# Weighing 64 of 128 value rows on ScalarE and GpSimd in a decode-attention kernel

## The chip, the core and the metric

The kernel runs on one core of a Trainium2 chip. The metric is the device time of one execution, in microseconds, as the median of three runs. The profiler recorded one execution, and every time quoted here comes from its page, its trace or from the times of the runs. Engines go by the profile's names: PE is TensorE, DVE is VectorE, ACT is ScalarE, POOL is GpSimd, SP is SyncE, which issues the loads.

## What is computed

One decoding step of an attention block with adaptive layer norms, followed by a small feed-forward block. Batch 4, one query per sequence, 32 heads of 128, 4096 cached positions, model width 512, feed-forward width 1792, all float32. The caches of keys and values are by far the largest inputs.

```
mod = (silu(c) @ w_mod).reshape(B, 6, 1, -1)          # sa, ca, ga, sb, cb, gb
h = layernorm(x) * (1 + ca) + sa
q = (h @ wq), split into 32 heads
scores = einsum("bhqd,bhkd->bhqk", q, k_cache) * Dh ** -0.5
p = softmax(scores)
o = einsum("bhqk,bhkd->bhqd", p, v_cache)
x = x + ga * (o @ wo)
h = layernorm(x) * (1 + cb) + sb
x = x + gb * (silu(h @ w1) @ w2)
```

## The kernel before

**Tiles.** A step `n` (0 to 31) handles one batch entry `b = n % 4` and a group `t = n // 4` of four heads. Its key tile and its value tile are 128 partitions by 128 rows by 128 columns (`NJ = 128`, `Dh = 128`): a partition holds 128 positions of one head, so each tile is 64 KiB per partition, 8.39 MB in all.

**Slots and loads.** All big tiles go through one pool, `kv`, with three slots taken in turn (class `Slot`). SP issues every load (`fetch`, L85), in the order of the program: key 0, key 1, value 0, key 2, value 1, key 3 and so on. So the load of key `n+2` takes the slot of value `n-1` and waits until that tile has been used up, and the load of value `n+1` takes the slot of key `n+1` and waits until DVE has reduced it.

**One step.** There is no scheduler: each engine's order is the order in which the loop (L434 to L475) is written, and semaphores do the rest.

- `mult`: the key tile is multiplied by the query, 40 rows on POOL and 88 on DVE (L280). DVE reads the query from PSUM, POOL a copy in SBUF that ACT makes (`make_qb`, L275).
- `vmult(n-1)`: of the value tile of the step before, POOL weighs the first 32 rows (`NV = 32`, L323) with the softmax weights in `sc` and adds them to four rows by halving (L327).
- `pv(n-1)`: PE handles the other 24 groups of four rows with weights that were placed in `pz` (L348), accumulating in `po`.
- `red`: DVE sums the products of the key tile along the columns (L285), 88 rows and then the 40 of POOL. This ends the use of the key tile.
- `rowmax`, `bmax`, `negmax`: the maximum per partition, then per head through a transpose on PE into a PSUM tile `mx`; DVE reduces it into a small SBUF tile `hx` (L298), masks it (L299) and sums it (L301).
- `vsum(n-1)`: PE adds POOL's four rows to `po` (L333). This ends the use of the value tile.
- `softexp(n)`: ACT takes the exponentials (L307) with their sums in `rs`, and POOL spreads the weights over `pz[0]` and `pz[1]` (L311).
- On the fourth step of a group (`b == 3`), `gather` (L359, L365) and `norm` follow: PE sums the denominators (L383 or L392) behind `vsum`, and DVE inverts them (L386, L387 in groups 0 to 3, L394 to L397 in groups 4 to 7). `gather(t-1, 1)` and `spread(t-1)` come on the second and third steps of the next group; `spread` ends with a copy into `oz` (L415) in groups 4 to 7.

The last two value tiles (`first(n) == 0`) go to PE whole. After the last step come the output projection (L423, L428), the second layer norm and the feed-forward block (L506, L516).

Of the kernel before, what the change touches and what calls it, by code (L numbers as in the profile page):

```python
# [9 lines left out]
F32 = mybir.dt.float32  # L10
AF = mybir.ActivationFunctionType
ALU = mybir.AluOpType
AX = mybir.AxisListType
# [4 lines left out]
def kernel(  # L18
# [10 lines left out]
    nc = tc.nc  # L29
    P = 128  # L30
    B, H, S, Dh = kc.shape
# [3 lines left out]
    W = P // G  # L35
    HP = 4
# [3 lines left out]
    TA = NT // 2  # L40
    QA = P // (HP * TA)
    RA = Dh // QA
    NJ = HP * S // P
    JJ = 4
    NG = NJ // JJ
    HG = NG // 2
# [4 lines left out]
    FG = F // G  # L51
    NA = 40
    NL = 56
    NV = 32
    SCALE = 1.0 / math.sqrt(Dh)
    EPS = 1e-5
    N = B * NT
# [4 lines left out]
    work = ctx.enter_context(tc.tile_pool(name="work", bufs=2))  # L62
# [3 lines left out]
    def psum(shape, tag, bufs):  # L66
        return ps.tile(shape, F32, tag=tag, name=tag, bufs=bufs)
# [19 lines left out]
    kt, vt = {}, {}  # L87
# [34 lines left out]
    ident = const.tile([P, P], F32, name="ident")  # L122
# [54 lines left out]
    oz = const.tile([P, NT - TA, R, B], F32, name="oz")  # L177
# [65 lines left out]
    for k in range(NK):  # L243
        for ch in range(H * Dh // CW):
            i, g = divmod(ch, G)
# [31 lines left out]
    sc, nm, po, rs = {}, {}, {}, {}  # L277
# [11 lines left out]
        nc.vector.tensor_reduce(nm[n], sc[n], axis=AX.X, op=ALU.max)  # L289

    def bmax(n):
        p = psum([P, P], "mx", 2)
        nc.tensor.transpose(p, nm[n].to_broadcast([P, P]), ident)  # L293
        nm[n] = p

    def negmax(n):
        m = work.tile([P, HP], F32, tag="hx", name=f"hx{n}")
        nc.vector.tensor_reduce(m, nm[n].rearrange("p (i x) -> p i x", i=HP), axis=AX.X, op=ALU.max)  # L298
        nc.vector.tensor_mul(m, m, hn)  # L299
        nm[n] = work.tile([P, 1], F32, tag="nm", name=f"nm{n}")  # L300
        nc.vector.tensor_reduce(nm[n], m, axis=AX.X, op=ALU.add)  # L301

    def softexp(n):
        t, b = divmod(n, B)
        if b == 0:
            rs[t] = work.tile([P, B], F32, tag="rs", name=f"rs{t}")
        nc.scalar.activation(sc[n], sc[n], AF.Exp, bias=nm[n], accum_out=rs[t][:, b : b + 1])  # L307
        for h in range(2):
            f = first(n) if h == 0 else 0
            m = HG - f  # L310
            nc.gpsimd.tensor_mul(  # L311
                pz[h][:, f * W : HG * W].rearrange("p (g x) -> p g x", g=m)[:, :, E:].rearrange("p g (i j) -> p g i j", i=HP),
                sc[n][:, JJ * (HG * h + f) : HG * JJ * (h + 1)].rearrange("p (g j) -> p g j", j=JJ)
                .unsqueeze(2).to_broadcast([P, m, HP, JJ]),
                hm.unsqueeze(1).unsqueeze(3).to_broadcast([P, m, HP, JJ]),
            )

    def first(n):
        return NV // JJ if n < N - 2 else 0

    def vmult(n):
        if first(n):
            nc.gpsimd.tensor_mul(  # L323
                vt[n][:, :NV, :], vt[n][:, :NV, :], sc[n][:, :NV].unsqueeze(2).to_broadcast([P, NV, Dh])
            )
            for m in (NV // 2, NV // 4, JJ):
                nc.gpsimd.tensor_add(vt[n][:, :m, :], vt[n][:, :m, :], vt[n][:, m : 2 * m, :])  # L327

    def vsum(n):
        t, b = divmod(n, B)  # L330
# [46 lines left out]
    rd = {}  # L377

    def norm(t):
        p = psum([P, B], "mx", 2)  # L380
        if t < TA:
            g = slice(W * t, W * (t + 1))
            nc.tensor.matmul(p[g], b8.rearrange("p i x -> p (i x)"), rs[t], start=True, stop=True)  # L383
            rd[t] = work.tile([P, B, QA], F32, tag="ra", name="ra", bufs=1)
            m = work.tile([P, B], F32, tag="dx", name="dx")
            nc.vector.reciprocal(m[g], p[g])  # L386
            nc.vector.tensor_mul(  # L387
                rd[t][g], m[g].unsqueeze(2).to_broadcast([W, B, QA]),
                dqm[g].unsqueeze(1).to_broadcast([W, B, QA]),
            )  # L390
            return
        nc.tensor.matmul(p, blk.rearrange("p i x -> p (i x)"), rs[t], start=True, stop=True)  # L392
        m = work.tile([P, B], F32, tag="dx", name="dx")
        nc.vector.tensor_mul(m, p, xm)  # L394
        rd[t] = work.tile([P, 2], F32, tag="rd", name="rd")
        nc.vector.tensor_reduce(rd[t][:, 0:1], m, axis=AX.X, op=ALU.add)
        nc.vector.reciprocal(rd[t][:, 1:2], rd[t][:, 0:1])  # L397

    def spread(t):
        if t < TA:  # L400
            g = slice(W * t, W * (t + 1))
            v = work.tile([P, B, QA, RA], F32, tag="o", name="v", bufs=1)
            nc.vector.tensor_mul(
                v[g], od[t][g].rearrange("p b (q r) -> p b q r", q=QA),
                rd[t][g].unsqueeze(3).to_broadcast([W, B, QA, RA]),
            )
            nc.vector.tensor_reduce(oa[g], v[g].rearrange("p b q r -> p r b q"), axis=AX.X, op=ALU.add)
            return
        on = work.tile([P, R, QW], F32, tag="lnu", name="on", bufs=1)
        nc.vector.tensor_scalar(  # L410
            on, od[t].rearrange("p (x r) -> p r x", r=R), rd[t][:, 1:2], None, op0=ALU.mult
        )
        ot = work.tile([P, R, W], F32, tag="o", name="ot", bufs=1)
        nc.vector.transpose(ot, on)
        nc.vector.tensor_copy(oz[:, t - TA], ot[:, :, :B])  # L415

    accp = psum([P, D], "acc", 1)
    nc.vector.memset(accp, 0.0)
# [15 lines left out]
    for n in range(N):  # L434
        t, b = divmod(n, B)
# [5 lines left out]
        w, m = (NJ // 2, NL // 2) if n == 0 else (NJ, NL) if n == 1 else (NJ, NA)  # L441
        for lo in range(0, NJ, w):
            mult(nc.gpsimd, qw, n, lo, lo + m)
            mult(nc.vector, qb, n, lo + m, lo + w)
            if n + 1 < N and not lo:
                make_qb(n + 1)
            if n:
                vmult(n - 1)
                pv(n - 1)
            red(n, lo + m, lo + w)  # L450
# [4 lines left out]
        else:  # L455
# [6 lines left out]
            fetch(s2.t, w12, 0, 3 * F, *(NK * F + i * D for i in (0, 5, 8, 10, 11, 12, 13, 14)))  # L462
        rowmax(n)
        bmax(n)
        if n and first(n - 1):
            vsum(n - 1)
        negmax(n)
        softexp(n)
        if b == 3:
            gather(t, 0)  # L470
            norm(t)
        if t and b == 1:
            gather(t - 1, 1)
        if t and b == 2:
            spread(t - 1)  # L475
    pv(N - 1)
    gather(NT - 1, 1)
    spread(NT - 1)
    project_a()
    project(TA, NT)  # L480
# [84 lines left out]
```

## Time and profile before

| What | Value |
|---|---|
| Median of three runs | 1319.33 us (1319.29 to 1319.63) |
| Profiled execution | 1319.24 us |
| Its span | 1317.5 us |
| Busy: DVE, POOL, PE, ACT | 1029.0, 848.6, 381.3, 51.4 us |
| Moved | 567.65 MB, 431 GB/s over the span |
| Granted PE clock, mean | 0.611 |

The profile's timelines give for each instruction its start and its length in microseconds, the engine, the line of the kernel, what it writes and reads, and in brackets how long the engine stood idle before it and what released it. The groups by shape give the count after an `x`, then the busy time, the mean length in ns, and the idle time ahead with its releasers. The rows of the windows give, for a stretch of time, the busy time of PE, its weight loads, DVE, ACT and POOL with the number of instructions, then the granted PE clock, the busy share of the DMA engines and the rate in GB/s.

### The profile page before, as it was taken

The page shows a single profiled execution, that of the slowest core. Times are in us where ns is not written, and L with a number is a line of the kernel's source. Part 1 is how long each engine was busy: PE and PEld are TensorE (multiplying, and loading weights), DVE is VectorE, ACT ScalarE, POOL GpSimd, SP SyncE. Part 2 cuts the span into 40 slices and gives each one's busy share as a digit, 9 for nine tenths or more (in the row PEclk, how much of TensorE's full clock was granted, in tenths as well). Part 3 has the DMA queues.
Part 4 walks back from the last instruction along what each step waited for, and adds up shares of the span by engine and source line. Part 5 has one row for each costly group of instructions (what it writes and reads, how often), then busy time and mean ns, then how long its engine had stood idle before and what let it go on. Part 6 is the DMA issues. An engine that isn't in the chain of part 4 may idle for free.

```text
span 1317.5 us, 5429 instructions
## 1 busy us (share of the span) xinstructions
PE 381.3 (29%) x2114; PEld 104.2 (8%) x2114; DVE 1029.0 (78%) x361; ACT 51.4 (4%) x164; POOL 848.6 (64%) x227
## 2 busy tenths in 40 slices
PE   3402333221222232133222123232312332221357
PEld 0100000000000000000000001000000000000013
DVE  2597788987877888788888887789887888977852
ACT  1100000000000000000000000000000000000001
POOL 0457767666876766687676677667667767666800
PEclk9756666655666665566665566666556666555668
DMA  9999999999999999999999999999999999999998
GB/s 414 436 422 446 434 424 442 422 440 442 420 442 432 432 438 434 434 436 428 436 438 430 430 440 434 430 436 438 426 438 438 428 432 438 434 432 438 428 428 344
DMA packets 11433, 567.65 MB, mean 431 GB/s; under 512 B 1280, under 2 KB 1296, under 8 KB 2192
## 3 DMA queue, kind: packets, MB, share of 16 engines
q1 hardware_dynamic: 11408, 567.31, 99.5%
q8 instruction: 17, 0.28, 0.1%
q14 instruction: 8, 0.07, 0.0%
HBM read 567.30 MB, written 0.01 MB: 431 GB/s over the span
## 4 chain that ended last, share of the span: by engine, by line
DMA 58%; DVE 25%; POOL 12%; PE 4%; issue 1%; ACT 0%; DVEq 0%; SPq 0%; POOLq 0%; ACTq 0%
DMA k<-in_A_k_cache_dram 31%; DMA v<-in_A_v_cache_dram 25%; DVE sc L285 14%; DVE k L280 10%; POOL v L327 6%; POOL v L323 5%; DMA wq<-in_A_wq_dram 3%; PE po L333 1%; PE po L348 1%; PE q L246 1%; PE acc L423 0%; PE q L506 0%; PE acc L428 0%; PE po L516 0%; PE mx L256 0%
## 5 line engine op out<-in xcount | busy, mean ns | idle before, releaser
L285 DVE TENSOR_REDUCE sc<-k 128x88 f32<-128x11264 f32 (+3 forms) x66 | 553.1, 8422 | 3.2
L280 DVE TENSOR_TENSOR k<-k,q 128x11264 f32<-128x11264 f32 (+2 forms) x33 | 376.3, 11402 | 169.8 <-DMA k<-in_A_k_cache_dram 155.5
L280 POOL TENSOR_TENSOR k<-k,qw 128x5120 f32<-128x5120 f32 (+2 forms) x33 | 361.8, 10964 | 123.5 <-DMA k<-in_A_k_cache_dram 92.1
L348 PE MATMUL po<-v,pz 128*32 128x512 f32 x1568 | 243.6, 786 | 645.4 <-DMA v<-in_A_v_cache_dram 645.4
L323 POOL TENSOR_TENSOR v<-v,sc 128x4096 f32<-128x4096 f32 x30 | 211.1, 7036 | 241.5 <-DMA v<-in_A_v_cache_dram 241.5
L327 POOL TENSOR_TENSOR v<-v 128x2048 f32<-128x2048 f32 (+2 forms) x90 | 243.5, 2705 | 7.1
L348 PEld LDWEIGHTS po<-v,pz 128*32 128x32 f32 x1568 | 64.7, 140 | 831.7 <-issue 831.7
L333 PE MATMUL po<-v,hs 128*32 128x512 f32 x60 | 57.4, 1060 | 140.6 <-POOL v L327 140.6
L311 POOL TENSOR_TENSOR pz<-sc,hm 128x128 f32<-128x128 f32 (+1 forms) x64 | 31.5, 514 | 33.7 <-ACT sc L307 33.7
L293 PE MATMUL mx<-ident,rm 128*128 128x128 f32 x32 | 11.3, 352 | 115.0 <-DVE rm L289 115.0
L307 ACT ACTIVATE sc<-sc,nm 128x128 f32<-128x128 f32 x32 | 12.8, 402 | 712.9 <-DVE nm L301 712.9
L275 ACT ACTIVATE qw<-q 128x128 f32<-128x128 f32 x32 | 8.9, 278 | 450.5 <-DVE k L280 417.4
L359 DVE TENSOR_TENSOR o<-po,jm 128x512 f32<-128x512 f32 x16 | 10.9, 682 | 14.6 <-PE po L348 14.6
L298 DVE TENSOR_REDUCE hx<-mx 128x4 f32<-128x128 f32 x32 | 9.3, 292 | 16.4 <-PE mx L293 16.4
L333 PEld LDWEIGHTS po<-v,hs 128*32 128x32 f32 x60 | 5.5, 141 | 147.3 <-POOL v L327 147.3
L365 DVE TENSOR_REDUCE s<-o 128x128 f32<-128x512 f32 x16 | 16.5, 1033 | 0.6
L299 DVE TENSOR_TENSOR hx<-hx,hn 128x4 f32<-128x4 f32 x32 | 16.0, 501 | 1.1
L293 PEld LDWEIGHTS mx<-ident,rm 128*128 128x128 f32 x32 | 4.7, 148 | 143.3 <-issue 112.3
L271 PE MATMUL q<-qm,blk 128*128 128x512 f32 x16 | 15.5, 1068 | 1.7 <-ACT qm L269 1.7
L199 PE MATMUL q<-wm 128*32 128x512 f32 x48 | 9.5, 698 | 18.9 <-DVE wm L183 18.9
L386 DVE RECIPROCAL dx<-mx 32x4 f32<-32x4 f32 x4 | 0.7, 179 | 16.7 <-PE po L333 11.9
L394 DVE TENSOR_TENSOR dx<-mx,xm 128x4 f32<-128x4 f32 x4 | 0.6, 162 | 15.7 <-PE mx L392 15.7
(113 smaller groups left out, 168.8 us busy)
## 6 DMA issues: line engine op xcount, KB each, us to landing
k<-in_A_k_cache_dram SPq DMA_DIRECT2D x2, 4096.0 KB, 51.9
wm<-in_head_dram SPq DMA_DIRECT2D x1, 6160.0 KB, 17.7
wo<-in_A_wo_dram SPq DMA_DIRECT2D x1, 4096.0 KB, 19.0
wo<-in_A_wo_dram SPq DMA_DIRECT2D x1, 3072.0 KB, 25.8
w<-in_B_w_dram SPq DMA_DIRECT2D x1, 2688.0 KB, 33.7
w<-in_B_w_dram SPq DMA_DIRECT2D x1, 1280.0 KB, 38.0
wo<-in_A_wo_dram SPq DMA_DIRECT2D x1, 1024.0 KB, 27.9
w<-in_B_w_dram SPq DMA_DIRECT2D x4, 256.0 KB, 17.5
```

The lines of the kernel that those rows point to most:

```text
L246: nc.tensor.matmul(pq[i][W * g : W * (g + 1), :], hT[:, k, :], wqt[:, k, ch * CW : (ch + 1) * CW], start=k == 0, stop=k == NK - 1,)
L271: nc.tensor.matmul(p, blk.rearrange("p i x -> p (i x)"), m, start=True, stop=True)
L280: eng.tensor_mul(kt[n][:, lo:hi, :], kt[n][:, lo:hi, :], src[n].unsqueeze(1).to_broadcast([P, hi - lo, Dh]))
L285: nc.vector.tensor_reduce(sc[n][:, lo:hi], kt[n][:, lo:hi, :], axis=AX.X, op=ALU.add)
L293: nc.tensor.transpose(p, nm[n].to_broadcast([P, P]), ident)
L299: nc.vector.tensor_mul(m, m, hn)
L311: nc.gpsimd.tensor_mul(pz[h][:, f * W : HG * W].rearrange("p (g x) -> p g x", g=m)[:, :, E:].rearrange("p g (i j) -> p g i j", i=HP), sc[n ...
L323: nc.gpsimd.tensor_mul(vt[n][:, :NV, :], vt[n][:, :NV, :], sc[n][:, :NV].unsqueeze(2).to_broadcast([P, NV, Dh]))
L327: nc.gpsimd.tensor_add(vt[n][:, :m, :], vt[n][:, :m, :], vt[n][:, m : 2 * m, :])
L333: nc.tensor.matmul(po[t, q][0:W, :], hs[:, o : o + W], vt[n][:, :JJ, :].rearrange("p j d -> p (j d)"), start=False, stop=a == 1,)
L348: nc.tensor.matmul(po[t, q][W * g : W * (g + 1), :], pz[h][:, o : o + W], vt[n][:, JJ * j : JJ * (j + 1), :].rearrange("p j d -> p (j d)") ...
L365: nc.vector.tensor_reduce(s, o.rearrange("p j d -> p d j"), axis=AX.X, op=ALU.add)
```

## The change

`NV` goes from 32 to 64. For thirty value tiles ACT now weighs rows 16 to 63, one row per instruction and in place (48 of 128x128), POOL rows 0 to 15 in one instruction. POOL then adds the seven further blocks of eight rows to the first, each in turn, and last the two halves of that block. PE keeps rows 64 to 127, 16 groups instead of 24. With 64 rows gone, `pz[0]` is not filled for these tiles. The small tile of the maximum becomes four more columns of the PSUM tile `mx`, the inverse of the denominators is written over the denominators in PSUM, and the copy into `oz` goes from DVE to ACT.

```diff
-    NV = 32
+    NV = 64
+    NC = 8
+    NP = 16
...
     def bmax(n):
-        p = psum([P, P], "mx", 2)
-        nc.tensor.transpose(p, nm[n].to_broadcast([P, P]), ident)
+        p = psum([P, P + HP], "mx", 2)
+        nc.tensor.transpose(p[:, :P], nm[n].to_broadcast([P, P]), ident)
         nm[n] = p
 
     def negmax(n):
-        m = work.tile([P, HP], F32, tag="hx", name=f"hx{n}")
-        nc.vector.tensor_reduce(m, nm[n].rearrange("p (i x) -> p i x", i=HP), axis=AX.X, op=ALU.max)
+        m = nm[n][:, P:]
+        nc.vector.tensor_reduce(m, nm[n][:, :P].rearrange("p (i x) -> p i x", i=HP), axis=AX.X, op=ALU.max)
...
         for h in range(2):
-            f = first(n) if h == 0 else 0
+            f = min(max(first(n) - HG * h, 0), HG)
             m = HG - f
+            if not m:
+                continue
...
     def vmult(n):
         if first(n):
+            v = vt[n]
+            for j in range(NP, NV):
+                nc.scalar.activation(v[:, j, :], v[:, j, :], AF.Copy, scale=sc[n][:, j : j + 1])
             nc.gpsimd.tensor_mul(
-                vt[n][:, :NV, :], vt[n][:, :NV, :], sc[n][:, :NV].unsqueeze(2).to_broadcast([P, NV, Dh])
-            )
-            for m in (NV // 2, NV // 4, JJ):
-                nc.gpsimd.tensor_add(vt[n][:, :m, :], vt[n][:, :m, :], vt[n][:, m : 2 * m, :])
+                v[:, :NP, :], v[:, :NP, :], sc[n][:, :NP].unsqueeze(2).to_broadcast([P, NP, Dh])
+            )
+            for lo in range(NC, NV, NC):
+                nc.gpsimd.tensor_add(v[:, :NC, :], v[:, :NC, :], v[:, lo : lo + NC, :])
+            nc.gpsimd.tensor_add(v[:, :JJ, :], v[:, :JJ, :], v[:, JJ:NC, :])
...
-            m = work.tile([P, B], F32, tag="dx", name="dx")
-            nc.vector.reciprocal(m[g], p[g])
+            nc.vector.reciprocal(p[g], p[g])
             nc.vector.tensor_mul(
-                rd[t][g], m[g].unsqueeze(2).to_broadcast([W, B, QA]),
+                rd[t][g], p[g].unsqueeze(2).to_broadcast([W, B, QA]),
...
-        nc.vector.tensor_copy(oz[:, t - TA], ot[:, :, :B])
+        nc.scalar.activation(oz[:, t - TA], ot[:, :, :B], AF.Copy)
```

The changed kernel's lines stand two further down from `NP` on, and seven further from `norm` on. POOL's order in the fourth step of a group, before: one key tile's part, the value tile, the placement of the weights, the next key tile's part.

```order
L280 TENSOR_TENSOR k_643<-k_643,qw_655 128x5120 [waits DMAHW2_49]
L323 TENSOR_TENSOR v_688<-v_688,sc_645 128x4096 [waits DMAHW3_49]
L327 TENSOR_TENSOR v_688<-v_688 128x2048 [waits Pool_49]
L327 TENSOR_TENSOR v_688<-v_688 128x1024 [waits Pool_49]
L327 TENSOR_TENSOR v_688<-v_688 128x512 [waits Pool_49]
L311 TENSOR_TENSOR pz_113<-sc_720,hm 128x8x16 [waits PE_49,Activation_49]
L311 TENSOR_TENSOR pz_114<-sc_720,hm 128x16x16 [waits PE_49]
L280 TENSOR_TENSOR k_718<-k_718,qw_723 128x5120 [waits DMAHW4_49]
```

The same place after the change:

```order
L282 TENSOR_TENSOR k_898<-k_898,qw_910 128x5120 [waits DMAHW2_49]
L330 TENSOR_TENSOR v_988<-v_988,sc_900 128x2048 [waits DMAHW3_49,DVE_49]
L334 TENSOR_TENSOR v_988<-v_988 128x1024 [waits Pool_49]
L334 TENSOR_TENSOR v_988<-v_988 128x1024 [waits Activation_49,Pool_49] x6
L335 TENSOR_TENSOR v_988<-v_988 128x512 [waits Pool_49]
L315 TENSOR_TENSOR pz_114<-sc_1017,hm 128x16x16 [waits PE_49,Activation_49]
L282 TENSOR_TENSOR k_1015<-k_1015,qw_1020 128x5120 [waits DMAHW4_49]
```

Six of the eight additions now wait for ACT as well as for the addition before, and one placement of weights is left. ACT's order at the same place before, where the exponential follows the copy of the query:

```order
L275 ACTIVATE qw_655<-q 128x128 [waits PE_49,Pool_49]
L307 ACTIVATE sc_645,rs_523<-sc_645,nm_698 128x128 [waits DVE_49,Pool_49]
L369 ACTIVATE mz<-s,am 128x128 [waits DVE_49,Activation_49]
L369 ACTIVATE mz<-s,am 128x128
L275 ACTIVATE qw_723<-q 128x128 [waits DVE_49,Pool_49]
L307 ACTIVATE sc_720,rs_767<-sc_720,nm_765 128x128 [waits DVE_49,Pool_49]
```

And after, with the value tile's 48 scalings ahead of each exponential:

```order
L277 ACTIVATE qw_910<-q 128x128 [waits PE_49,Pool_49]
L329 ACTIVATE v_882<-v_882,sc_802 128x128 [waits DMAHW6_49,DMAHW1_49,Activation_49]
L329 ACTIVATE v_882<-v_882,sc_802 128x128 x47
L309 ACTIVATE sc_900,rs_693<-sc_900,nm_997 128x128 [waits DVE_49,Pool_49]
L377 ACTIVATE mz<-s,am 128x128 [waits DVE_49,Activation_49]
L377 ACTIVATE mz<-s,am 128x128
L277 ACTIVATE qw_1020<-q 128x128 [waits DVE_49,Pool_49]
```

The exponential and the two scalings for `gather` stand behind a wait for the value tile. PE at the end of the fourth step before:

```order
L293 MATMUL mx<-ident,rm_690 128x128 [waits DVE_49,PE_49]
L333 MATMUL po<-v_625,hs 32x512 [waits Pool_49]
L370 MATMUL od<-mz,s_124 32x256 [waits PE_49,Activation_49]
L383 MATMUL mx<-rs_523,b_120 32x4 [waits PE_49]
L348 MATMUL po<-v_688,pz_113 32x512 [waits DMAHW3_49,Pool_49]
```

It is the same after, but for the names and that the value groups begin with `pz_114`: the denominators (L383, now L391) stand behind L333, now L341, which waits for POOL. On SP the order of the loads is the same; a key load now waits for ACT besides PE.

## The prediction

> **What bounds the kernel now.** I read the page first: the span, the busy shares and the DMA queues.
>
> ```profile
> span 1317.5 us, 5429 instructions
> PE 381.3 (29%) x2114; PEld 104.2 (8%) x2114; DVE 1029.0 (78%) x361; ACT 51.4 (4%) x164; POOL 848.6 (64%) x227
> q1 hardware_dynamic: 11408, 567.31, 99.5%
> 60.00:1240.00 1180.00, 313.32 (x1587) 79.70 (x1587) 969.46 (x281) 38.06 (x136) 826.88 (x214) 0.59 1.00 434
> ```
>
> No engine is full, but the loading queue is busy 99.5% of the span; the last row, from the table of windows, shows DMA share 1.00 and 434 GB/s from 60 to 1240 us. So compute costs time only where it makes a load start so late that the queue runs dry. The kernel streams 32 key and 32 value tiles through three slots, so the question is how early each load is issued. SP's timeline around the fourth tile of a head group, then GpSimd's, ScalarE's and DVE's rows from theirs:
>
> ```profile
> 493.57 0.33 SPq L85 DMA_DIRECT2D v<-in_A_v_cache_dram  x1
> 500.95 0.33 SPq L85 DMA_DIRECT2D k<-in_A_k_cache_dram  x1
> 532.25 0.33 SPq L85 DMA_DIRECT2D v<-in_A_v_cache_dram  x1
> ...
> 483.57 7.04 POOL L323 TENSOR_TENSOR v<-v,sc 128x4096 f32<-128x4096 f32 x1 [8.27 <-DMA v<-in_A_v_cache_dram]
> 490.68 8.27 POOL L327 TENSOR_TENSOR v<-v 128x2048 f32<-128x2048 f32 x3
> 502.94 11.03 POOL L280 TENSOR_TENSOR k<-k,qw 128x5120 f32<-128x5120 f32 x1 [3.06 <-DMA k<-in_A_k_cache_dram]
> 522.24 7.04 POOL L323 TENSOR_TENSOR v<-v,sc 128x4096 f32<-128x4096 f32 x1 [8.28 <-DMA v<-in_A_v_cache_dram]
> ...
> 495.49 0.40 ACT L307 ACTIVATE sc<-sc,nm 128x128 f32<-128x128 f32 x1 [30.96 <-DVE nm L301]
> ...
> 493.57 0.29 DVE L289 TENSOR_REDUCE rm<-sc 128x1 f32<-128x128 f32 x1
> ...
> 501.04 0.18 DVE L386 RECIPROCAL dx<-mx 32x4 f32<-32x4 f32 x1 [3.98 <-PE po L333]
> 501.26 0.18 DVE L387 TENSOR_TENSOR ra<-dx,dqm 32x32 f32<-32x32 f32 x1
> 502.95 11.89 DVE L280 TENSOR_TENSOR k<-k,q 128x11264 f32<-128x11264 f32 x1 [1.51 <-DMA k<-in_A_k_cache_dram]
> 514.94 17.28 DVE L285 TENSOR_REDUCE sc<-k 128x88 f32<-128x11264 f32 x2
> ...
> 541.59 11.89 DVE L280 TENSOR_TENSOR k<-k,q 128x11264 f32<-128x11264 f32 x1 [7.51 <-DMA k<-in_A_k_cache_dram]
> ```
>
> Call the landing of a value tile T: GpSimd starts it at 483.57. A key tile lands at T+19.4 (502.95), the next value tile at T+38.7 (522.24). Two loads wait on compute:
>
> - The key load at 500.95 needs the slot of the value tile of T, so it waits for GpSimd's sums and PE's last matmul (L333). It stands behind the value load issued at 493.57, whose bytes land at 522.24. So it is issued 21.3 us before the queue could run dry.
> - The value load at 532.25 needs DVE's last reduction of a key tile. The transfer ahead of it lands at 541.59, so its lead is 9.3 us. This is the tight one, and DVE sets it.
>
> How much lead does a transfer need? An upper and a lower bound come from the first and the last DMA of the kernel:
>
> ```profile
> wm<-in_head_dram SPq DMA_DIRECT2D x1, 6160.0 KB, 17.7
> out_dram<-w SPq DMA_DIRECT2D x1, 8.0 KB, 1.8
> ```
>
> The 8 KB one takes 1.8 us from issue to landing. The head's 6.31 MB at 434 GB/s would take 14.5 us and takes 17.7, so 3.2 us lie around it. A lead of over 3.2 us costs nothing; between 1.8 and 3.2 it is open. I take 1.8: nothing else is on the queue for that DMA, while the head's 3.2 holds the kernel's own start.
>
> **The change, part by part.** Durations come from the groups kept apart by shape:
>
> ```profile
> L323 POOL TENSOR_TENSOR v<-v,sc 128x4096 f32<-128x4096 f32 x30 | 211.1, 7036 | 241.5 <-DMA v<-in_A_v_cache_dram 241.5
> L327 POOL TENSOR_TENSOR v<-v 128x1024 f32<-128x1024 f32 x30 | 70.3, 2344 | 2.4
> L327 POOL TENSOR_TENSOR v<-v 128x512 f32<-128x512 f32 x30 | 37.9, 1263 | 2.4
> L269 ACT ACTIVATE qm<-qn,sel 128x128 f32<-128x128 f32 x32 | 10.2, 389 | 8.2 <-DVE oa L407 4.8 <-DVE oz L415 3.3
> L299 DVE TENSOR_TENSOR hx<-hx,hn 128x4 f32<-128x4 f32 x32 | 16.0, 501 | 1.1
> L394 DVE TENSOR_TENSOR dx<-mx,xm 128x4 f32<-128x4 f32 x4 | 0.6, 162 | 15.7 <-PE mx L392 15.7
> ```
>
> GpSimd, per value tile. Before: 7.04 + 0.07 + 8.27 = 15.4 us. After: 16 rows weighed, half of 7.04, 3.5; seven additions of 128x1024 at 2.344, 16.4; one of 128x512, 1.3; eight gaps of 0.07, 0.6. Together 21.8 us, 6.4 more. The smaller placement of the weights (one multiplication, not two) stands behind it.
>
> ScalarE, per value tile: 48 scalings of 128x128. L269 is the same operation with a column as its scale: 10.2 us busy for 32, so 0.319 each back to back, 15.3 us; alone 0.389, 18.7 us. GpSimd takes eight rows every 2.4 us and first works 5.9 us on its own 16, so its last addition of eight could begin at T+18.1; the last rows are ready at T+15.3, or T+18.7 at the slow end. The sums then end at T+21.8, or 18.7+2.34+0.07+1.26 = T+22.4. I take 21.8, since the scalings stand together as in L269's busy time. A lower end: none of GpSimd's rows can go faster than the same shapes went, so 21.8 it is.
>
> What waits for that? The exponential (L307) stands behind the 48 on ScalarE: T+11.9 (495.49) becomes T+15.3 to 18.7, still ahead of GpSimd's end, and only the placement of weights and the denominators need it. GpSimd's part of the next key tile starts at about T+22.6, not T+19.4, and ends at T+33.7; DVE needs it after 11.9 + 11.9 us of its own work, at T+43. GpSimd is free five us before the next value tile (T+38.7). The key load moves from T+17.4 to T+23.8, and its lead from 21.3 to 14.9 us: far above 3.2. SP's queue is otherwise in the same order, and the loads behind it were issued later in any case.
>
> PE: 16 groups for 24, off the path. The scratch tiles in PSUM: L299 takes 0.50 us on two SBUF operands, L394 0.16 with one in PSUM, so some 0.34 x 32 = 11 us of DVE go, all after the reduction that releases the load: zero on the path (between 0 and the same 0.34 late, if PSUM gave nothing). The copy of `oz` moves to ScalarE. The one near the end of the kernel, from its timeline:
>
> ```profile
> 1289.41 5.31 PE L423 MATMUL acc<-wo,oa 128*4 128x512 f32 x32
> ...
> 1290.26 0.17 DVE L415 COPY oz<-ot 128x16 f32<-128x16 f32 x1
> ```
>
> Even at ScalarE's 0.389 it is done by 1290.7, and its reader comes behind L423, at 1294.7: zero again, and 0.2 us if that cover were gone.
>
> The fourth tile of each group is the one to look at. There DVE waits for the denominators (L386, or L394 in the second half), which PE forms behind L333, and so behind GpSimd:
>
> ```profile
> 967.42 0.16 DVE L397 RECIPROCAL rd<-rd 128x1 f32<-128x1 f32 x1
> 968.02 11.89 DVE L280 TENSOR_TENSOR k<-k,q 128x11264 f32<-128x11264 f32 x1 [0.43 <-DMA k<-in_A_k_cache_dram]
> ```
>
> Before, DVE was through 1.5 us (501.44) or 0.4 us (967.58) ahead of the next key tile. With 6.4 us added it comes 4.9 us late in four groups and 6.0 in three (the last group has nothing behind it). DVE then does 11.9 + 17.3 us without a pause, so the value load's lead falls from 9.3 to 4.4 and 3.4 us. Both are over 3.2. DVE had 7.5 us of idle time ahead of the following key tile (541.59), so it catches up within one tile. What is late next is nothing that empties the queue.
>
> The sum on the path is zero. The profiled execution took 1319.24 us (1.74 around the span), 0.09 under the median of the runs; I predict 1319.3.
>
> Does more traffic slow the stream itself? Two windows, one without PE, one with its heaviest use of value tiles:
>
> ```profile
> 540.00:560.00 20.00, 0.00 (x0) 0.00 (x0) 18.31 (x2) 0.28 (x1) 11.03 (x1) 0.50 1.00 433
> 560.00:580.00 20.00, 10.21 (x53) 2.43 (x53) 13.79 (x8) 1.19 (x4) 16.09 (x6) 0.67 1.00 433
> ```
>
> Both moved 433 GB/s. ScalarE is nearly idle in both, so for its 48 rows this is only the nearest row. [...]
>
> **The rivals.** Slower: the late value load on the fourth tile. If the sums end e us later than T+21.8, the leads are 3.4-e (three tiles) and 4.4-e (four). With a need of 1.8 it costs 2.6 us from e = 2.5 on; with 3.2, from e = 1.1. At e = 2.5 the larger need gives 3 x 2.3 + 4 x 1.3 = 12 us. So 1322 to 1331, with 1326 in the middle. For it: the slow end of the scalings alone gives e = 0.6, and waits between ScalarE and GpSimd for every eight rows are not in any row. Against it: those waits lie under GpSimd's own additions until e is used up.
>
> [...]
>
> Faster: the stream speeds up, since PE reads 16 groups of a value tile for 24. A gain of 0.2% (2.6 us, about what a measurement of this kernel can tell from no change) needs 435 GB/s for 434 all through, 1316.6. The two windows speak against it. [...]
>
> **How the numbers follow.** No change, 1319.3 within 2.6 either way: 0.75. The late load: 0.12. Contention: 0.04. Faster: 0.09. So same 0.75, slower 0.16, faster 0.09. The range goes from 1317.0, above which nearly all of the first case lies, to 1325, which takes in the smaller half of the late load and the contention case.
>
> **What would show it.** Right: L330 to L335 end near 21.8 us after a value tile lands, ScalarE's 48 take 15 us, DVE's key multiplication on fourth tiles starts 5 to 6 us after the landing, the value load after it keeps a lead of over 3 us, DMA share stays 1.00 at 434 GB/s, and DVE's busy time falls by some 10 us. Wrong: a DMA share under 1.00 after fourth tiles, seven dents in all, or a lower rate everywhere while ScalarE works.

## The result, and the profile after

The changed kernel took 1326.81 us (median of six runs, 1324.72 to 1328.51) against 1319.36 us before (1319.14 to 1319.63): 1.0055 times the time, 95% interval 1.0044 to 1.0066. So it is 7.4 us slower, outside the forecast range of 1317.0 to 1325.0, and on the side to which I had given 0.16. Its runs also scatter over 3.8 us, where those of the kernel before lie within 0.5 in this comparison.

The profiled execution is the fastest of the six, 1324.72 us. Its page, the span, the busy shares and the DMA queues:

```profile
span 1322.7 us, 6268 instructions
PE 328.4 (25%) x1634; PEld 87.7 (7%) x1634; DVE 1013.8 (77%) x357; ACT 472.2 (36%) x1608; POOL 1022.1 (77%) x347
q1 hardware_dynamic: 11408, 567.31, 99.5%
q8 instruction: 13, 0.21, 0.1%
q14 instruction: 22, 0.18, 0.0%
```

The queue that carries the tiles is as busy as before, 99.5%, with the same 11408 packets, and still takes longer. The line that changed unnoticed is the last: queue q14, which the page lists as instruction, has 22 packets where the kernel before had this:

```profile
q8 instruction: 17, 0.28, 0.1%
q14 instruction: 8, 0.07, 0.0%
```

Now the fourth step of the third group, as in the prediction. From the timelines of the changed kernel, ACT, POOL, DVE and SP in turn:

```profile
484.83 14.14 ACT L329 ACTIVATE v<-v,sc 128x128 f32<-128x128 f32 x48 [12.34 <-DMA v<-in_A_v_cache_dram]
...
484.89 3.61 POOL L330 TENSOR_TENSOR v<-v,sc 128x2048 f32<-128x2048 f32 x1 [5.20 <-DMA v<-in_A_v_cache_dram]
488.58 16.94 POOL L334 TENSOR_TENSOR v<-v 128x1024 f32<-128x1024 f32 x7
505.61 1.26 POOL L335 TENSOR_TENSOR v<-v 128x512 f32<-128x512 f32 x1
...
508.95 0.20 DVE L393 RECIPROCAL mx<-mx 32x4 f32<-32x4 f32 x1 [10.78 <-PE po L341]
509.40 11.89 DVE L282 TENSOR_TENSOR k<-k,q 128x11264 f32<-128x11264 f32 x1
521.42 17.28 DVE L287 TENSOR_REDUCE sc<-k 128x88 f32<-128x11264 f32 x2
...
542.79 11.89 DVE L282 TENSOR_TENSOR k<-k,q 128x11264 f32<-128x11264 f32 x1 [2.43 <-DMA k<-in_A_k_cache_dram]
...
494.87 0.33 SPq L87 DMA_DIRECT2D v<-in_A_v_cache_dram  x1
508.90 0.33 SPq L87 DMA_DIRECT2D k<-in_A_k_cache_dram  x1
538.73 0.33 SPq L87 DMA_DIRECT2D v<-in_A_v_cache_dram  x1
```

The compute terms came close to what was worked out: the sums end 22.0 us after the landing (forecast 21.8), DVE's reciprocal now waits 10.78 us for PE instead of 3.98, and the value load at 538.73 goes out 4.1 us before the key tile ahead of it lands at 542.79 (forecast 4.4, before 9.3). What did not hold is that this costs nothing. Of the signs that the prediction named for being wrong, the dents behind fourth tiles are there, if shallow: in seven windows of 20 us around these loads (220 to 240, 375 to 395, and so on to 1155 to 1175 us) the rate is 396 to 426 GB/s, against 423 to 455 in the kernel before, and the DMA share 0.95 to 1.00 against 0.98 to 1.05.

### The profile page after: what moved, and what is told of

Read it like the earlier page. It is cut to its first block, busy times and chain, and to the rows that moved or that the text cites. A ratio compares the mean times of both kernels' runs of the same rounds, so it can differ in the third digit from the quotient of the medians.

```text
span 1322.7 us, 6268 instructions
## 1 busy us (share of the span) xinstructions
PE 328.4 (25%) x1634; PEld 87.7 (7%) x1634; DVE 1013.8 (77%) x357; ACT 472.2 (36%) x1608; POOL 1022.1 (77%) x347
## 3 DMA queue, kind: packets, MB, share of 16 engines
q1 hardware_dynamic: 11408, 567.31, 99.5%
## 4 chain that ended last, share of the span: by engine, by line
DMA 49%; DVE 29%; POOL 18%; PE 3%; issue 1%; ACT 0%; POOLq 0%; SPq 0%; DVEq 0%
DMA v<-in_A_v_cache_dram 22%; DMA k<-in_A_k_cache_dram 21%; DVE sc L287 17%; POOL v L334 14%; DVE k L282 12%; DMA w<-in_B_w_dram 3%; POOL v L330 3%; DMA wq<-in_A_wq_dram 3%; PE po L341 2%; POOL v L335 1%; PE q L248 1%; PE mx L258 0%; PE od L378 0%; PE od L383 0%; ACT qm L271 0%
## 5 line engine op out<-in xcount | busy, mean ns | idle before, releaser
L334 POOL TENSOR_TENSOR v<-v 128x1024 f32<-128x1024 f32 x210 | 494.0, 2352 | 16.5
L329 ACT ACTIVATE v<-v,sc 128x128 f32<-128x128 f32 x1440 | 424.1, 387 | 214.5 <-DMA v<-in_A_v_cache_dram 214.5
L356 PE MATMUL po<-v,pz 128*32 128x512 f32 x1088 | 191.1, 868 | 450.8 <-DMA v<-in_A_v_cache_dram 450.8
L330 POOL TENSOR_TENSOR v<-v,sc 128x2048 f32<-128x2048 f32 x30 | 108.4, 3612 | 156.2 <-DMA v<-in_A_v_cache_dram 156.2
L341 PE MATMUL po<-v,hs 128*32 128x512 f32 x60 | 57.4, 1060 | 302.2 <-POOL v L335 302.2
L356 PEld LDWEIGHTS po<-v,pz 128*32 128x32 f32 x1088 | 48.4, 152 | 599.6 <-issue 581.6
L315 POOL TENSOR_TENSOR pz<-sc,hm 128x256 f32<-128x256 f32 x34 | 20.8, 615 | 30.7 <-ACT sc L309 30.7
L335 POOL TENSOR_TENSOR v<-v 128x512 f32<-128x512 f32 x30 | 38.1, 1268 | 2.4
L341 PEld LDWEIGHTS po<-v,hs 128*32 128x32 f32 x60 | 5.4, 140 | 310.2 <-POOL v L335 310.2
L300 DVE TENSOR_REDUCE mx<-mx 128x4 f32<-128x128 f32 x32 | 9.6, 299 | 18.4 <-PE mx L295 18.4
```

The source lines that it names most:

```text
L315: nc.gpsimd.tensor_mul(pz[h][:, f * W : HG * W].rearrange("p (g x) -> p g x", g=m)[:, :, E:].rearrange("p g (i j) -> p g i j", i=HP), sc[n ...
L329: nc.scalar.activation(v[:, j, :], v[:, j, :], AF.Copy, scale=sc[n][:, j : j + 1])
L330: nc.gpsimd.tensor_mul(v[:, :NP, :], v[:, :NP, :], sc[n][:, :NP].unsqueeze(2).to_broadcast([P, NP, Dh]))
L334: nc.gpsimd.tensor_add(v[:, :NC, :], v[:, :NC, :], v[:, lo : lo + NC, :])
L335: nc.gpsimd.tensor_add(v[:, :JJ, :], v[:, :JJ, :], v[:, JJ:NC, :])
L341: nc.tensor.matmul(po[t, q][0:W, :], hs[:, o : o + W], vt[n][:, :JJ, :].rearrange("p j d -> p (j d)"), start=False, stop=a == 1,)
```

## The experiments

Each was compared with runs of the kernel before on the same chip (medians 1319.36 to 1319.47). Theory A: the late value load on fourth steps empties part of the queue. Theory B: the added data traffic of ACT and POOL in SBUF slows the stream. Theory C came up after the first four runs.

**Undo the wait on fourth steps.** `norm` of a group moves to the first step of the next one, behind DVE's key multiplication; everything else is as in the changed kernel.

```diff
+            if t and b == 0:
+                norm(t - 1)
             if n:
                 vmult(n - 1)
...
             gather(t, 0)
-            norm(t)
+            if t == NT - 1:
+                norm(t)
```

> The changed kernel with norm of groups 0 to 6 moved to the first step of the next group, behind DVE's key multiplication, so that on fourth steps DVE no longer waits for GpSimd's sums through PE; ScalarE's 48 scalings and GpSimd's additions stay. Theory A (on fourth steps DVE comes 5 to 6 us late to the key tile, so the value load after it is issued only 3.3 to 4.2 us ahead of the end of the transfer before it, and the queue runs partly dry): the lead is back near 9 us and the time is 1319.4, within 1 us. Theory B (ScalarE's and GpSimd's added traffic in SBUF slows the stream): nothing of that is gone, so 1325 to 1328 as in the changed kernel.

1323.54 us, ratio 1.0032 (1.0020 to 1.0043): neither theory's time. From its DVE timeline:

```profile
503.89 11.89 DVE L282 TENSOR_TENSOR k<-k,q 128x11264 f32<-128x11264 f32 x1 [5.96 <-DMA k<-in_A_k_cache_dram]
515.81 0.20 DVE L393 RECIPROCAL mx<-mx 32x4 f32<-32x4 f32 x1
```

DVE is ready 6 us ahead of the key tile, and the wait for PE is gone: the value loads of fourth steps go out 8.8 to 9.6 us ahead of the landing before them. Yet 4.2 us remain, and they are not a lower rate throughout. Landings of successive value tiles, from POOL's timeline:

```profile
367.48 3.61 POOL L330 TENSOR_TENSOR v<-v,sc 128x2048 f32<-128x2048 f32 x1 [5.09 <-DMA v<-in_A_v_cache_dram]
406.77 3.61 POOL L330 TENSOR_TENSOR v<-v,sc 128x2048 f32<-128x2048 f32 x1 [5.79 <-DMA v<-in_A_v_cache_dram]
445.37 3.61 POOL L330 TENSOR_TENSOR v<-v,sc 128x2048 f32<-128x2048 f32 x1 [5.10 <-DMA v<-in_A_v_cache_dram]
484.65 3.61 POOL L330 TENSOR_TENSOR v<-v,sc 128x2048 f32<-128x2048 f32 x1 [5.76 <-DMA v<-in_A_v_cache_dram]
523.24 3.61 POOL L330 TENSOR_TENSOR v<-v,sc 128x2048 f32<-128x2048 f32 x1 [5.08 <-DMA v<-in_A_v_cache_dram]
```

The intervals are 39.29, 38.60, 39.28 and 38.59 us. The time is lost in steps of 0.68 us, ten of them from the eighth tile on, 2.2 tiles apart on average, with undisturbed intervals between (38.6 us, or 19.30 from any big tile to the next). By theory B every interval in which ACT works would be longer. The ten steps make 6.9 us. That is more than 4.2, because the kernel before loses some 2.5 us against 19.30 us per tile itself, in one step of 1.6 us and many small ones; most of this does not come on top of the ten.

The trace keeps, for every transfer, sixteen completion marks, and for every packet its queue and time; it names the DMA engine of neither. The profile counts 16 DMA engines, so I read each mark as one engine's. A tile has landed with its last mark: in the kernel before, POOL starts on the value tile of T at 483.57, 0.07 us behind the last mark (483.50) and 2.3 us behind the first (481.23). The marks show what is late (times moved to the span's start, to some 0.1 us):

```
norm moved:     q14 packet at   371.8   450.1   539.6   644.0   721.9   802.3
next landing to jump           387.34  465.22  543.09  659.57  737.52  815.39
16th mark behind the 15th       0.73    1.33    1.92    2.43    3.12    3.71
kernel before, landing         386.91  464.19  541.46  657.42  734.70  813.48
16th mark behind the 15th       0.11    0.11    0.11    0.11    0.11    1.62
```

The last mark falls behind the other fifteen by a further 0.6 to 0.7 us at the first landing after such a packet, at most 16 us later, and wins back some 0.1 us at most before the next step of the table. All ten steps follow a q14 packet in this way. The other twelve of the 22 packets show no step at the landings; by my reading they delay an engine whose mark is not the last. Theory C, my explanation, is that ACT's instructions come 8 KB at a time through one of the engines that carry the tiles, and that a tile has landed only when the slowest engine is through. That q14's packets have 8 KB and that a landing is the last mark is in the trace; which engine a packet goes through is not.

**Delay DVE in the kernel before.** One DVE reduction with an unused result goes behind `norm` on the fourth steps of groups 0 to 6; ACT and POOL are as before. The number of columns was 47, 70 and, later, 35.

```diff
             gather(t, 0)
             norm(t)
+            if t < NT - 1:
+                dl = work.tile([P, 47], F32, tag="dl", name="dl", bufs=1)
+                nc.vector.tensor_reduce(dl, ident.unsqueeze(1).to_broadcast([P, 47, P]), axis=AX.X, op=ALU.max)
```

> The kernel before, with one extra DVE reduction of about 6.4 us behind norm on the fourth steps of groups 0 to 6 (reads ident, its result is not used). ScalarE and GpSimd do what they did before. Theory A: leads of 4.4 and 3.4 us as in the changed kernel, so 1323 to 1329. Theory B: 1319.4, since there is no added traffic of ScalarE or GpSimd.

> The same with about 9.6 us of extra DVE time: leads of about 1.2 us in four groups and 0.2 us in three. Theory A: every one of the seven value loads starts late, by 3 to 5 us, so 1335 to 1350. Theory B: 1319.4 if leads do not matter as long as they are positive.

> The kernel before with about 4.8 us of extra DVE time behind norm on fourth steps of groups 0 to 6, between the 0 of the kernel before and the 6.4 that cost 6.2 us: leads of about 6.0 us in four groups and 4.9 in three. Theory A with a need near 4 to 4.5 us (1.8 us from issue to data, and 2 to 3.7 us by which the first of the sixteen DMA engines is through ahead of the last): 1319.4 to 1320.5. If the loss grew with every microsecond of delay, about three quarters of 6.2: 1324.

With 6.4 us: 1325.55, ratio 1.0045 (1.0030 to 1.0060). With 9.6 us: 1338.73, 1.0142 (1.0125 to 1.0159). With 4.8 us: 1320.10, 1.0002 (0.9993 to 1.0011). From SP's and DVE's timelines with 6.4 us:

```profile
538.74 0.33 SPq L85 DMA_DIRECT2D v<-in_A_v_cache_dram  x1
...
502.99 6.42 DVE L474 TENSOR_REDUCE dl<-ident 128x47 f32<-128x6016 f32 x1
509.44 11.89 DVE L280 TENSOR_TENSOR k<-k,q 128x11264 f32<-128x11264 f32 x1
...
543.11 11.89 DVE L280 TENSOR_TENSOR k<-k,q 128x11264 f32<-128x11264 f32 x1 [2.77 <-DMA k<-in_A_k_cache_dram]
```

The same 4.4 us of lead as forecast for the changed kernel, without any of its traffic, go with a loss of 6.2 us. In the profiled executions, leads of 5.1 to 6.7 us (4.8 us of delay) cost nothing, and leads of 3.6 to 5.5 us (6.4 of delay) made the seven value tiles land 0.4 to 1.0 us late, 4.8 us together. With 9.6 us of delay the seven cost 0.6 to 2.2 us each, less than the 3 to 5 expected, and 10.8 together; 8.4 us more were lost at seven key tiles, each behind a q8 packet (see the last section). The extra reduction by itself is no rival, since 4.8 us of it cost nothing. So theory A holds, with a need near 5 us where I had 1.8, and at most 3.2.

The completion marks suggest why. In the kernel before, the first mark comes some 2.3 us ahead of the last from 250 to 790 us, and 3.7 us later on. A landing is the last mark; if each mark is one engine's, the first engine has by then been without work for that long if the next load is late. To the 1.8 us from issue to landing of the small DMA come these 2.3 to 3.7, which makes 4.1 to 5.5. This sum is an estimate of when the first engine runs out of work. Why the last mark is then late too, which alone moves the landing, no run shows. Nor is the point sharp: in the changed kernel three of the seven late tiles, with leads of 3.2 to 4.1 us by the marks, landed after an undisturbed interval, and the other four, with 3.3 to 3.9, 0.5 to 2.0 us late.

**Two thirds of ACT's rows.**

> The changed kernel with NV = 48: ScalarE weighs 32 rows, GpSimd 16 rows and five additions of eight, so the sums end 4.7 us earlier, about 17.1 us after the landing, against 15.4 before and 21.8 in the changed kernel. Theory A: on fourth steps DVE comes no more than 1.3 us late, leads of 8 to 9 us, so 1319.4 within 1 us. Theory B: two thirds of ScalarE's scalings are left, so about two thirds of the loss, 1324.

1321.57 us, ratio 1.0017 (1.0008 to 1.0026). Between the two forecasts: the late load is gone, and the landings show seven steps of 0.7 to 0.9 us about three tiles apart, at 19 packets on q14. With 32 ACT instructions per tile instead of 48 the steps come less often: seven, against ten at 22 packets with `norm` moved.

**Instructions without data.** To the kernel before, 48 or 96 one-column ACT instructions per value tile are added; nothing reads what they write.

```diff
+            if n and first(n - 1):
+                tn = work.tile([P, 96], F32, tag="tn", name="tn", bufs=1)
+                for i in range(48):
+                    nc.scalar.activation(tn[:, i : i + 1], epst, AF.Copy)
             if n:
                 vmult(n - 1)
```

> The kernel before, with 48 more ScalarE instructions of one column each per value tile (they copy a constant into a scratch tile that nothing reads; ScalarE has the time for them). As many instructions as the changed kernel gives ScalarE, next to no data. Theory C (ScalarE's instructions are fetched from memory, 8 KB at a time, by one of the sixteen DMA engines that carry the tiles; each fetch puts this engine about 0.68 us behind, and a tile has landed only when the last engine is through): some fourteen more fetches, the first three or so absorbed, 1323 to 1324.5, as with norm moved. Theory B (the data that ScalarE moves slows the stream): 1319.4.

> The same with 96 such instructions per value tile. Theory C: some 28 more fetches, 1330 to 1335. Theory B: 1319.4.

1323.13 us, ratio 1.0029 (1.0018 to 1.0040), and 1334.24 us, 1.0108 (1.0093 to 1.0123). The pages have, for 48 and for 96:

```profile
q14 instruction: 19, 0.16, 0.0%
```

```profile
q14 instruction: 31, 0.25, 0.0%
```

1440 instructions bring 11 packets and 3.7 us; 2880 bring 23 and 14.8 us. Per packet that is 0.33 and then 0.64 us. In the profiled executions the landings show 11 steps with 48 instructions (7.6 us, nine of the steps behind a q14 packet) and 25 with 96 (17.7 us). The times differ by less, since the 2.5 us that the kernel before loses itself no longer come on top, and since both executions landed their second key tile 1.0 us earlier than the kernel before did.

**Data without instructions.** ACT writes the 48 rows with one instruction (one scale for all), with `norm` moved and without:

```diff
-            for j in range(NP, NV):
-                nc.scalar.activation(v[:, j, :], v[:, j, :], AF.Copy, scale=sc[n][:, j : j + 1])
+            nc.scalar.activation(v[:, NP:NV, :], v[:, NP:NV, :], AF.Copy, scale=sc[n][:, 0:1])
```

> The changed kernel with norm moved, and ScalarE's 48 rows of a value tile written by one instruction with one scale for all of them (this leaves out the weighing row by row); the same data pass through ScalarE. Theory C: 1319.4 within 0.7, since the fetches are gone. Theory B: 1323.5, as with norm moved alone.

> The changed kernel with norm where it was, and ScalarE's 48 rows in one instruction as in the run above (the weighing row by row is left out). Only the late value load of fourth steps is left. Theories A and C together: 1322 to 1326, near the 1325.6 of the kernel with DVE's extra 6.4 us; theory C alone without A: 1319.4.

With `norm` moved: 1319.83 us, ratio 1.0002 (0.9992 to 1.0011); its page has these two lines:

```profile
PE 327.9 (25%) x1634; PEld 87.7 (7%) x1634; DVE 1013.2 (77%) x357; ACT 214.8 (16%) x198; POOL 1021.1 (78%) x347
q14 instruction: 9, 0.07, 0.0%
```

The rows pass through ACT and POOL adds them just as long (1021.1 us busy), and the whole 4.2 us are gone with the instructions, within the interval. Theory B falls, and theory C has its test from both sides, except for the engine that a packet goes through, which no run shows. Without moving `norm`: 1325.57 us (four runs, 1324.72 to 1329.60), 1.0042 (1.0025 to 1.0059), which is the late load alone.

**The small tiles alone, and a try at a faster kernel.**

> The kernel before with only the small tiles of the maximum and of the denominators in PSUM and the copy into oz on ScalarE; the value tiles as before. Every theory: 1319.4 within 0.5, since DVE's 11 us saved lie behind the reduction that releases the load.

> A try at a faster kernel: norm moved and the PSUM tiles as in the changed kernel, but GpSimd alone weighs and adds 48 rows (one multiplication, four additions, about 24 us), no scalings on ScalarE, four PE groups fewer per tile than before. Theory A and C: neither late loads nor added fetches, two of PE's seventeen fetches fewer, so 1318 to 1319.5; a gain, if any, is under 0.1%. Anything above 1321 would say that GpSimd's longer sums cost in another way.

The PSUM tiles alone: 1319.26 us, ratio 0.9998 (0.9989 to 1.0007). POOL alone on 48 rows, with `norm` moved: 1319.31, 0.9998 (0.9989 to 1.0007). In the latter POOL works 23.4 us on a value tile:

```profile
484.04 10.46 POOL L326 TENSOR_TENSOR v<-v,sc 128x6144 f32<-128x6144 f32 x1 [3.42 <-DMA v<-in_A_v_cache_dram]
494.58 12.86 POOL L330 TENSOR_TENSOR v<-v 128x3072 f32<-128x3072 f32 x4
```

That is longer than in the changed kernel and costs nothing, as no fourth step waits for it. It gains nothing either: none of these versions beats the kernel before.

## Why the prediction was wrong

- **What bounds the kernel** was right: the stream does. Its row of the page is the same after, 99.5%, which also shows that this row does not tell whether time is lost. That compute costs time only through late loads was wrong: with `norm` moved no value load is late, and 4.2 us are lost.
- **POOL's and ACT's terms** were right: 22.0 us for 21.8, and ACT's 48 in 14.14 for 15.3.
- **The leads on fourth steps** were right, 4.1 us measured in the third group for 4.4.
- **"A lead of over 3.2 us costs nothing"**, with 1.8 taken for the need, is the step that failed first. It took the latency of one transfer into an empty queue for the need. The sixteen marks of the head's load come within 1.2 us of each other, and those of the tiles of the kernel before within 2.3 to 3.7, which the bound left out. The runs put the need near 5 us, and the price at 6.1 to 6.2 us (1325.57 and 1325.55). The rival had the place and the direction, 1322 to 1331, but it was to cost 2.6 us only with sums that end 1.1 to 2.5 us after T+21.8, and they ended 0.2 us after it; so it got 0.12.
- **A term was missing altogether.** The change gives ACT 1440 instructions more, and I costed what they do, not the q14 packets that come with them, 22 for 8. With the late loads out of the way that term is 4.2 us (1323.54), and 3.7 us for bare instructions in the kernel before. The page before had the row, q14 with 8 packets and 0.0%; the prediction has no term for it, and gave 0.75 to no change.
- The two prices do not add: 4.2 and 6.1 us alone, 7.4 together. The marks of the changed kernel suggest why. The distance from first to last mark falls from 2.9 to 2.0 us with the late tile that lands at 718 us, and from 3.0 to 1.2 at 1030, and both land in time. My reading is that, where the queue runs partly dry, the engines ahead wait and the engine that lags catches up. At four of the seven late tiles the distance grows instead (from 1.4 to 2.7 us at 253), so this reading holds for part of them at most, and was not tested by itself.
- **Contention** was rightly given little. No run shows the contention case that the top of the range, 1325, takes in: with ACT's data and without its instructions the kernel takes 1319.83 us, ratio 1.0002 (0.9992 to 1.0011), no loss that can be measured. Instructions with next to no data are another matter: 1323.13 us with 48 per value tile and 1334.24 with 96.
- **DVE's gain** was real and worth nothing, as forecast. From the groups by shape of the changed kernel, where L301 is the former L299:

```profile
L301 DVE TENSOR_TENSOR mx<-mx,hn 128x4 f32<-128x4 f32 x32 | 5.5, 170 | 1.1
```

  10.5 of DVE's 15.2 us less come from this line (16.0 before), and the small tiles alone moved the time by -0.2 us, within the interval.

One sum of the prediction is off by little, and nothing hangs on it: 9.3 less 6.0 is a lead of 3.3 us, not 3.4.

## What to carry to other kernels

In a kernel whose loading queue is busy 99.5% of the span, as here, do not take one transfer's latency (1.8 us) for the lead that a load needs: add the distance between the first and the last completion mark (2.3 to 3.7 us). Here that makes about 5 us, as an estimate; leads of 5.1 to 6.7 us cost nothing (1320.10 us), and leads of 3.6 to 5.5 cost 6.2 us (1325.55). Count instructions as well as their work: here 1440 small instructions on ACT cost 3.7 us with next to no data, and came with 11 more packets on q14. And a DMA share of 99% does not say that nothing was lost: the queue was busy 99.5% in the profiled executions of 1319.24 and of 1324.72 us. Look at the intervals between landings.

## What the hardware showed unexpectedly

- One more 8 KB packet on q14 came with every 125 to 131 instructions added to ACT (2880 with 23, 1440 with 11). A packet takes 0.31 us by its record, and where a step follows it in the run with `norm` moved, the landing moved by 0.68 us. What makes up the rest is open.
- The other instruction queue, q8, has 17 packets of 16 KB in the kernel before and 13 in the changed kernel, where PE does less (1634 instructions for 2114); so I take it for PE's. The landing intervals of the kernel before show no steps beside them but one: 1.6 us, at 813 us (1.5 with 4.8 us of delay). The marks come later behind them all the same. At each of the 13 key tiles that land 12 to 17 us after a q8 packet, from 155 to 1238 us, the sixteen marks, summed, come 1.6 to 2.8 us later than 19.30 us after those before (at the other tiles 1.2 at most), but only at 813 us does the last mark move by more than 0.1 us. Where the marks lie close together, with 9.6 us of delay (first to last 0.4 to 0.9 us at the late tiles), the landing moved by 0.7 to 1.6 us behind seven such packets. In these runs a late mark cost time where it was the last one; with `norm` moved, that is so behind ten of q14's 22 packets.
- DMA share and rate can hide a loss. With `norm` moved the stretch from 60 to 1240 us reads as in the kernel before, and the kernel is 4.2 us slower, while fifteen marks run ahead of the one that sets the landings, by 4.4 us at the last tile:

```profile
60.00:1240.00 1180.00, 262.22 (x1105) 64.21 (x1105) 953.85 (x278) 457.85 (x1579) 992.54 (x329) 0.57 1.00 434
```
